# Batch 1's softmax denominators by VectorE's 32x32 turns, in a fused attention and channel-mix kernel with all steps placed anew

## The chip, the cores and the metric

The kernel runs on one core of one Trainium2 chip. The metric is device time in microseconds for one launch, as the median of the runs shown. One further execution was profiled; it has a time of its own.

## What is computed

Eight batches, eight heads, 576 tokens, 64 values a head and 32 memory slots. The reference, cut to what matters:

```python
a = exp(phi - max(phi)); a = a / (sum(a) + 1e-9)          # over the 32 slots
k_m = einsum('bhsm,bhsd->bhmd', a, k)
v_m = einsum('bhsm,bhsd->bhmd', a, v)
scores = q @ k_m.T / sqrt(64)
attn = exp(scores - max(scores)); attn = attn / (sum(attn) + 1e-9)
x = attn @ v_m                                            # heads side by side: 8 x 576 x 512
xk = mu_k * x + (1 - mu_k) * x_prev                       # x_prev: the token before
xr = mu_r * x + (1 - mu_r) * x_prev
h = maximum(xk @ w_k, 0)                                  # 512 -> 1024
out = sigmoid(xr @ w_r) * ((h * h) @ w_v)                 # 1024 -> 512, float32
```

## The kernel before

All work is cut into small steps, and `PLAN` (lines 19 to 39) is a list of them written out by hand, one word for a step. At line 591 the words are turned into calls in exactly that order, so each engine gets its instructions in the order in which the words stand. An instruction that waits holds those behind it on its engine. There is no loop over batches that sets the order: the list mixes steps of several batches.

A word `b:name` is a step of batch `b`. `exp` (L226) is ScalarE's exponential of phi. `z` (L248) sums it over tokens with matmuls and takes the reciprocal. `k`, `v`, `kv` (L238) are the 36 or 72 small matmuls that gather k and v into the 32 slots. `nk`, `nv`, `hn` (L275, L286) scale them, `tk`, `ht` (L307) transpose the keys, `q0`, `q1`, `qh0`, `qh1` (L325) turn q by VectorE in 32x32 blocks, `s` (L340, L345) makes the scores and their exponentials `e`. A number after `exp`, `hn`, `ht`, `qh`, `s`, or a `c` after `k0`, `v0`, picks one half of the heads or of the rows.

Then come the softmax denominators, in one of two ways. The first way has four `l` steps (L355 to L360): a matmul of `e` with a block matrix of ones, `sumh`, sums over the 32 slots of each head and leaves the sum on all 32 rows, and ScalarE takes Ln of it. `h0z` to `h3z` or `r0z`, `r1z` (L365) then take Exp of minus that, which is the reciprocal. The second way has three VectorE steps: `fe` (L370) turns `e` in 32x32 blocks, `fs` (L376, L377) adds over the 32 slots and takes reciprocals, and `fo` (L382) turns these back, each repeated 32 times. In both ways `y0` to `y3` or `w0`, `w1` (L389) multiply `e` by the result. Batches 4 to 7 take the second way before the change, batches 0 to 3 the first.

For batches 2 to 7, `x0`, `x1` make the attention output and `dd`, `k0d`, `r0d` and others mix each token with the one before on VectorE and ScalarE. For batches 0 and 1 the mix is folded into the values instead: `nk0`, `nr0`, `nk1`, `nr1` (L435) scale the values by mu (spread over rows by `mub`, L201 to L205), and `mk0`, `mk1`, `mr0`, `mr1` (L444 to L452) make the mixed inputs by matmuls straight into PSUM. ScalarE and VectorE share their copies out.

The channel mix: `cN:f` (L525 to L533) is one 128-wide block of keys for chunk N of tokens: four matmuls, a relu by ScalarE, a square by VectorE. `g:t` (L548, L553) is the gate of 128 tokens and its exponential. `sg:p` (L559, L560) finishes the sigmoid of two such tiles on ScalarE. `o:t` (L574, L576) is the value product of 128 tokens, VectorE's product with the gate, and the store that SP's queue issues. Chunk 0 and the value tiles 0 to 3 go in halves `a` and `b`.

`0:busyN` issues N matmuls on zeros (L196), whose result nothing reads. The words `p:...` and `b:load` issue loads; all but the first phi go through POOL's queue, in the order of the words. `p:k:0a` and the identity (`PRE`) stand ahead of the list. `b:load` loads batch b+2, and does nothing for 6 and 7. All PSUM tiles share eight banks; `sg` has two buffers, `rl` three.

Of the kernel before, what the change touches and what calls it, by code (L numbers as in the profile page):

```python
# [16 lines left out]


PLAN = [
    "p:k:0b 0:exp0 0:exp1 0:mub 0:mu 0:z 0:k1c 0:k0c 0:hn0 0:hn1 p:q:0a 0:qh0 0:ht0 p:q:0b p:v:0b 0:qh1 0:ht1 p:v:0a",  # L20
    "0:s0 0:l0 0:h0z 0:s1 0:l1 0:v0c 0:y0 0:v1c 0:nr0 0:nk1 0:h1z 0:l2 0:l3 0:nr1 p:wk:4-8 0:h3z 0:y1 0:h2z 0:y3 0:y2",
    "0:busy9 0:nk0 p:wk:0-4 0:mk1 p:phi:1 0:mk0 c0:3b p:wr:0-4 0:mr0 1:exp 0:mr1 c0:3a c0:6b c0:1b c0:4a g:3 c0:2a",
    "c0:5b p:k:1 g:1 g:2 1:k 1:z 1:nk p:q:1 1:q0 sg:1 1:q1 c0:7b c0:6a p:v:1 c0:7a 1:tk g:0 c0:0a c0:0b c0:5a 1:s",
    "c0:2b 1:v c0:1a 1:l2 1:l1 c0:4b 1:h2z 1:nk0 1:h1z p:wv:0-2 1:l3 1:l0 1:y2 p:wv:2-4 1:nr0 1:nr1 o:2a 1:h0z 1:y1",
    "1:h3z sg:0 1:nk1 1:y0 o:3a 1:y3 o:3b o:2b 1:mk1 0:load o:0a 1:mk0 1:mr0 2:exp c1:0 c1:3 g:4 c1:1 1:mr1 c1:7 g:5",
    "2:z sg:2 2:kv 2:nk 2:q1 2:q0 c1:2 2:tk 2:nv 1:load 2:load c1:4 c1:5 o:1b 3:exp c1:6 2:s o:5 2:l1 2:l0 2:l2 2:l3",
    "2:r1z 2:w1 2:r0z 2:w0 3:z o:0b o:4 3:kv 3:nk 3:nv 2:x0 g:7 g:6 3:tk 3:q1 2:x1 3:q0 2:dd sg:3 o:1a g:8 2:k0d",
    "2:k2d 3:s 4:exp o:7 o:6 3:l1 3:l0 2:r0d 7:load 3:l2 c2:2 3:l3 c2:3 3:r0z 3:w0 3:r1z 3:w1 c2:6 c2:0 c2:1 c2:5 4:z",
    "3:x1 2:r2d 4:q1 4:kv 4:ak c2:4 c2:7 3:x0 4:q0 3:load g:9 sg:4 5:exp 3:dd 4:tk 4:av 3:k2d o:8 o:9 3:k0d g:12 g:10",
    "5:z 3:r2d 3:r0d 5:q0 4:s 5:kv 5:ak 4:fe 5:av 5:q1 g:11 c3:3 c3:0 sg:5 4:fs 5:load 7:exp c3:7 4:fo c3:6 4:w0",  # L30
    "4:load c3:4 g:13 4:w1 o:10 c3:2 sg:6 c3:5 7:z c3:1 o:11 4:x0 g:14 7:kv 4:x1 7:ak 7:q0 7:q1 g:15 5:tk 4:dd o:12",
    "4:k2d sg:7 5:s 4:k0d 6:exp o:13 g:16 5:fe 5:fs g:17 5:fo c4:1 7:tk sg:8 o:15 7:av c4:6 c4:5 5:w0 c4:0 c4:3 5:w1",
    "6:z 6:q0 4:r2e 7:s c4:4 7:fe 6:load c4:2 c4:7 o:14 4:r0e 5:x0 o:17 6:kv 6:ak 7:fs 5:x1 5:dd 6:q1 g:18 g:19 sg:9",
    "o:16 5:k0d 6:av g:21 g:20 6:tk 5:k2d 5:r2e o:19 6:s o:18 6:fe 5:r0e 6:fs c5:4 6:fo c5:2 c5:1 sg:10 g:23 6:w1",
    "c5:0 c5:3 6:w0 c5:6 g:22 c5:5 c5:7 6:x1 7:fo o:20 7:w1 6:x0 7:w0 sg:11 o:21 6:dd g:25 6:k2d 6:k0d 7:x1 o:22 7:x0",
    "7:dd 6:r2e o:23 7:k2d g:24 sg:12 6:r0e c6:3 c6:2 c6:4 7:k0d c6:5 g:26 c6:7 c6:0 c6:6 c6:1 g:27 c7:1 c7:6 c7:0",
    "o:24 c7:7 o:25 g:29 7:r2e sg:13 c7:5 7:r0e o:26 c8:4 c8:3 c7:4 c8:5 c8:6 c7:3 g:28 c7:2 o:27 c8:1 sg:14 g:30",
    "g:31 sg:15 o:31 c8:0 o:30 g:32 g:33 o:28 sg:16 c8:2 o:29 c8:7 o:33 g:35 g:34 sg:17 o:32 o:34 o:35",
]

LOADS = {None: ("phi", "k", "v", "q")}
# [589 lines left out]
```

## Time and profile before

| what | us |
|---|---|
| runs shown | 203.63, 204.36, 205.88 (median 204.36) |
| the profiled execution's own time | 204.69 |
| its span, first to last instruction | 202.9 |
| TensorE busy | 188.7 |
| VectorE busy | 143.2 |
| ScalarE busy | 159.9 |
| nine matmuls of `busy9`, from 16.28 | 4.05 |
| first matmul of `mk1` | 20.26 |
| last value tile's matmuls end, in the chain | 199.22 |

The span is measured on the core from its first to its last instruction; the time of the execution holds 1.8 us more. The profile's page has the share of each engine, the span in 40 slices, and the chain of work that ended last. Other views give groups of instructions by line and shape, a timeline, the chain in order of time, busy time in chosen stretches, and for each load the time from its issue to its landing. Matmuls overlap in the records, so the busy time of a group of them is more than the time it keeps the engine.

### The profile page before, as it was taken

How to read it: one execution, taken by the hardware profiler on the slowest of the kernel's cores; microseconds unless marked ns; L12 is line 12 of the kernel's file. 1: busy time of each engine (PE TensorE's matmuls, PEld its weight loads, DVE VectorE, ACT ScalarE, POOL GpSimd, SP SyncE). 2: the span in 40 equal slices, each digit the busy share in tenths (PEclk: the TensorE clock that was granted, in tenths of full speed). 3: DMA queues.
4: the chain of work that ended last, by engine and by line, in shares of the span. 5: the costliest groups of instructions: out<-in, count | busy, mean ns of one | idle time of the engine just before them, and what ended most of it. 6: DMA issues, size and time to landing. Idle time of an engine off the chain costs nothing.

```text
span 202.9 us, 5384 instructions
## 1 busy us (share of the span) xinstructions
PE 188.7 (93%) x2174; PEld 97.5 (48%) x2174; DVE 143.2 (71%) x344; ACT 159.9 (79%) x318; POOL 29.5 (15%) x45
## 2 busy tenths in 40 slices
PE   0459999999999999999999999999999999999992
PEld 0324666755565454544446844444444444444451
DVE  2275746775748999999899989898999732713422
ACT  2235989988968999999999889988999739697360
POOL 7643222201504010036000000000000000000000
PEclk9999999999999999999999999999999999999998
DMA  6999999999999999999999213240422022223435
GB/s 162 169 207 263 209 208 198 267 222 292 212 274 238 243 294 222 240 147 204 257 245 232 60 25 82 52 103 3 103 57 52 3 54 50 52 52 89 98 86 144
DMA packets 24537, 31.29 MB, mean 154 GB/s; under 512 B 1968, under 2 KB 19648, under 8 KB 24512
## 3 DMA queue, kind: packets, MB, share of 16 engines
q0 software_dynamic: 17392, 20.91, 55.4%
q1 hardware_dynamic: 6352, 9.19, 17.9%
q10 hardware_dynamic: 768, 0.85, 1.3%
q8 instruction: 17, 0.28, 0.6%
q14 instruction: 8, 0.07, 0.1%
HBM read 38.28 MB, written 9.44 MB: 235 GB/s over the span
## 4 chain that ended last, share of the span: by engine, by line
PE 91%; DMA 3%; DVE 2%; ACT 1%; issue 1%; POOL 1%; POOLq 0%; DVEq 0%
PE pv L574 31%; PE pk L525 31%; PE pr L548 16%; PE kvps L238 4%; DMA kv<-in_k_dram 3%; PE scps L340 2%; PE idle L196 2%; PE nops L294 2%; PE mxps L294 1%; PE zps L355 1%; PE zps L248 1%; DVE qT L325 1%; DVE o L576 0%; PE ktps L307 0%; ACT e L345 0%
## 5 line engine op out<-in xcount | busy, mean ns | idle before, releaser
L525 PE MATMUL pk<-xkT,wk 128*128 128x512 bf16 (+4 forms) x352 | 68.4, 340 | 0.2 <-ACT xkT L452 0.2
L574 PE MATMUL pv<-wv,sq 128*128 128x512 bf16 (+1 forms) x328 | 67.8, 353 | 0.3 <-DVE sq L533 0.3
L529 ACT ACTIVATE rl<-pk 128x512 bf16<-128x512 f32 (+3 forms) x80 | 41.7, 559 | 10.2 <-PE pk L525 9.0
L525 PEld LDWEIGHTS <-wk 128*128 128x128 bf16 x352 | 33.2, 98 | 28.6 <-issue 1.0
L574 PEld LDWEIGHTS <-sq 128*128 128x128 bf16 x328 | 30.8, 98 | 29.6 <-issue 1.1
L533 DVE TENSOR_TENSOR sq<-rl 128x512 bf16<-128x512 bf16 (+5 forms) x104 | 31.6, 336 | 17.6 <-ACT rl L529 16.9
L576 DVE TENSOR_TENSOR o<-sg,pv 128x512 f32<-128x512 f32 (+1 forms) x41 | 24.9, 616 | 16.1 <-PE pv L574 11.2
L548 PE MATMUL pr<-wr,xrT 128*128 128x512 bf16 x144 | 35.5, 379 | 0.1
L553 ACT ACTIVATE sg<-pr 128x512 f32<-128x512 f32 x36 | 21.2, 609 | 7.0 <-PE pr L548 5.3
L548 PEld LDWEIGHTS <-xrT 128*128 128x128 bf16 x144 | 13.5, 98 | 15.8 <-ACT xrT L452 0.4
L560 ACT ACTIVATE sg<-sg 128x1024 f32<-128x1024 f32 x18 | 19.0, 1058 | 0.6
L559 ACT ACTIVATE sg<-sg 128x1024 f32<-128x1024 f32 x18 | 19.1, 1059 | 0.3
L401 ACT CAST x<-nops 128x320 bf16<-128x320 f32 (+1 forms) x48 | 15.7, 421 | 2.7 <-PE nops L294 2.6
L345 ACT ACTIVATE e<-scps 128x288 bf16<-128x288 f32 x32 | 10.6, 415 | 6.7 <-PE scps L340 6.6
L389 DVE TENSOR_TENSOR atn<-e,lz 128x576 bf16<-128x576 bf16 (+2 forms) x20 | 12.3, 632 | 3.4 <-ACT lz L365 3.4
L325 DVE STREAM_TRANSPOSE qT<-q 128x576 uint32<-128x576 uint32 (+1 forms) x16 | 13.1, 835 | 0.3 <-DMA q<-in_q_dram 0.3
L427 DVE TENSOR_TENSOR xrT<-x,mu_d 128x1152 bf16<-128x1152 bf16 x12 | 9.0, 751 | 3.7 <-ACT mu_d L424 3.4
L424 ACT ACTIVATE mu_d<-diff,mu 128x576 bf16<-128x576 bf16 x16 | 11.6, 783 | 0.0
L226 ACT ACTIVATE em<-ph 128x1152 bf16<-128x1152 f32 (+1 forms) x9 | 9.5, 1061 | 2.5 <-DMA ph<-in_phi_dram 2.5
L238 PE MATMUL kvps<-kv,em 64*32 64x128 bf16 (+1 forms) x720 | 8.6, 218 | 2.2 <-DMA kv<-in_k_dram 2.2
L426 DVE TENSOR_SCALAR mu_d<-diff,mu 128x576 bf16<-128x576 bf16 x32 | 10.2, 362 | 0.0
L238 PEld LDWEIGHTS <-em 64*32 64x32 bf16 x720 | 7.2, 93 | 4.8 <-issue 4.3
(65 smaller groups left out, 146.1 us busy)
## 6 DMA issues: line engine op xcount, KB each, us to landing
out_dram<-o SPq DMA_DIRECT2D x61, 128.0 KB, 2.4
ph<-in_phi_dram POOLq DMA_DIRECT2D x7, 576.0 KB, 17.2
kv<-in_k_dram POOLq DMA_DIRECT2D x7, 576.0 KB, 17.1
q<-in_q_dram POOLq DMA_DIRECT2D x7, 576.0 KB, 19.4
kv<-in_v_dram POOLq DMA_DIRECT2D x7, 576.0 KB, 19.7
out_dram<-o SPq DMA_DIRECT2D x18, 64.0 KB, 5.6
wk<-in_moe_w_k_dram POOLq DMA_DIRECT2D x2, 512.0 KB, 12.6
wv<-in_moe_w_v_dram POOLq DMA_DIRECT2D x2, 512.0 KB, 21.1
```

The costliest lines, as they stand in the source:

```text
L238: nc.tensor.matmul(kvps[c][g * M:(g + 1) * M], lhsT=em[ROWS[c], j, g, :], rhs=kv5[ROWS[c], parts, g, j, :], start=j == 0, stop=j == NJ - 1 ...
L325: nc.vector.transpose(dst.bitcast(U32), src.bitcast(U32))
L401: nc.scalar.copy(st["x"][:, i, sl], pss[i])
L525: nc.tensor.matmul(pk[:, p0 - lo:p1 - lo], lhsT=wk_sb[:, di, fi * 128:(fi + 1) * 128], rhs=xk_T[:, di, p0 % RING:p0 % RING + p1 - p0], sta ...
L529: nc.scalar.activation(rl, pk, AF.Relu)
L533: nc.vector.tensor_mul(sq[:, fi, p:p + p1 - p0], rl[:, p0 - lo:p1 - lo], rl[:, p0 - lo:p1 - lo])
L548: nc.tensor.matmul(pr, lhsT=xr_T[:, di, c0:c0 + 128], rhs=wr_sb[:, di, :], start=(di == 0), stop=(di == ND - 1))
L553: nc.scalar.activation(sg[:, t % 2], pr, AF.Exp, scale=-1.0)
L559: nc.scalar.activation(gated[p], gated[p], AF.Ln, bias=1.0)
L560: nc.scalar.activation(gated[p], gated[p], AF.Exp, scale=-1.0)
L574: nc.tensor.matmul(pv[:, cols], lhsT=sq[:, fi, p:p + 128], rhs=wv_sb[:, fi, cols], start=(fi == 0), stop=(fi == NF - 1))
L576: nc.vector.tensor_mul(o[:, cols], gated[t // 2][:, t % 2, cols], pv[:, cols])
```

## The change

Batch 1's four `l` and four `hNz` steps are gone, and `1:fe`, `1:fs`, `1:fo` stand in the list instead; its `y0` to `y3` stay. `0:busy9` has become `0:busy4`. All the other words are the same ones, in a new order. Nothing but `PLAN` is touched. The list at its start and its end:

```diff
-    "p:k:0b 0:exp0 0:exp1 0:mub 0:mu 0:z 0:k1c 0:k0c 0:hn0 0:hn1 p:q:0a 0:qh0 0:ht0 p:q:0b p:v:0b 0:qh1 0:ht1 p:v:0a",
-    "0:s0 0:l0 0:h0z 0:s1 0:l1 0:v0c 0:y0 0:v1c 0:nr0 0:nk1 0:h1z 0:l2 0:l3 0:nr1 p:wk:4-8 0:h3z 0:y1 0:h2z 0:y3 0:y2",
-    "0:busy9 0:nk0 p:wk:0-4 0:mk1 p:phi:1 0:mk0 c0:3b p:wr:0-4 0:mr0 1:exp 0:mr1 c0:3a c0:6b c0:1b c0:4a g:3 c0:2a",
-    "c0:5b p:k:1 g:1 g:2 1:k 1:z 1:nk p:q:1 1:q0 sg:1 1:q1 c0:7b c0:6a p:v:1 c0:7a 1:tk g:0 c0:0a c0:0b c0:5a 1:s",
-    "c0:2b 1:v c0:1a 1:l2 1:l1 c0:4b 1:h2z 1:nk0 1:h1z p:wv:0-2 1:l3 1:l0 1:y2 p:wv:2-4 1:nr0 1:nr1 o:2a 1:h0z 1:y1",
-    "1:h3z sg:0 1:nk1 1:y0 o:3a 1:y3 o:3b o:2b 1:mk1 0:load o:0a 1:mk0 1:mr0 2:exp c1:0 c1:3 g:4 c1:1 1:mr1 c1:7 g:5",
...
-    "o:24 c7:7 o:25 g:29 7:r2e sg:13 c7:5 7:r0e o:26 c8:4 c8:3 c7:4 c8:5 c8:6 c7:3 g:28 c7:2 o:27 c8:1 sg:14 g:30",
-    "g:31 sg:15 o:31 c8:0 o:30 g:32 g:33 o:28 sg:16 c8:2 o:29 c8:7 o:33 g:35 g:34 sg:17 o:32 o:34 o:35",
+    "0:exp0 p:k:0b p:q:0b 0:exp1 0:k0c 0:z 0:hn0 p:q:0a p:phi:1 1:exp 0:k1c 0:ht0 p:v:0b 0:mu p:v:0a 0:mub 0:hn1",
+    "0:qh1 0:ht1 0:s1 0:qh0 0:s0 0:v1c 0:l0 0:v0c 0:nk0 0:h0z 0:l1 0:y0 1:z 0:l3 0:l2 0:nk1 0:busy4 0:nr1 0:nr0 0:h1z",
+    "0:y1 0:h3z 0:h2z p:k:1 0:y3 0:y2 0:mk1 0:mk0 p:wk:4-8 p:wk:0-4 1:k 1:nk p:q:1 p:wr:0-4 0:mr1 c0:5a c0:6a c0:7b",
+    "0:mr0 p:wv:2-4 c0:3a c0:1b p:v:1 1:tk c0:3b c0:7a 1:q1 c0:6b p:wv:0-2 1:q0 c0:0b c0:4a 0:load c0:1a c0:2a c0:4b",
+    "1:s 1:fe 1:fs c0:0a g:1 c0:2b 1:fo g:0 c0:5b sg:0 g:3 g:2 1:y1 sg:1 2:exp o:1b 1:v 1:nr0 1:nr1 1:y0 1:y2 1:nk0",
+    "1:y3 o:3b 1:nk1 7:load o:2b o:3a o:2a 1:mr0 1:mk1 g:5 2:z 1:load 1:mk0 g:4 c1:3 c1:7 c1:4 c1:5 sg:2 2:kv 2:nk",
+    "2:nv 1:mr1 2:q0 2:q1 c1:1 2:tk c1:0 c1:2 c1:6 2:s o:4 2:l3 2:l2 2:l1 2:l0 2:r1z 2:w1 2:load 2:r0z 2:w0 o:0a",
...
+    "7:r2e o:27 o:26 c7:1 c7:4 o:24 c8:0 c8:3 c8:6 c7:2 g:28 c8:4 g:31 g:30 g:29 sg:14 c8:5 c8:1 o:29 c8:2 o:28 g:32",
+    "g:33 c8:7 sg:16 o:32 o:33 g:35 sg:15 o:31 g:34 sg:17 o:30 o:34 o:35",
```

## The prediction

> **What bounds the kernel now.** I read the busy table first, then the slices, then the chain of waits, because a busy share alone doesn't say whether an engine sets the end.
>
> ```profile
> PE 188.7 (93%) x2174; PEld 97.5 (48%) x2174; DVE 143.2 (71%) x344; ACT 159.9 (79%) x318; POOL 29.5 (15%) x45
> PE   0459999999999999999999999999999999999992
> PE 91%; DMA 3%; DVE 2%; ACT 1%; issue 1%; POOL 1%; POOLq 0%; DVEq 0%
> ```
>
> TensorE is full from the fourth slice (15 us) to the last, and the chain is TensorE for 91%. So a change can gain in two ways only: less work on TensorE, or fewer places where it stood still or did nothing of use. The chain in order of time (start, length, what) shows both near its start:
>
> ```profile
> 16.49 3.84 PE idle L196 x9
> 20.33 0.43 PE mxps L294 x13
> 20.76 0.37 ACT xkT L452
> ...
> 36.30 0.27 ACT rl L529
> 36.57 0.07 issue
> 36.63 0.71 ACT lz L360 x2
> 37.34 0.29 ACT rl L529
> 37.62 0.02 issue
> 37.65 0.30 DVE sq L533
> ```
>
> 3.84 us are filler (busy9). After it, useful work runs from 20.33 to the last matmul's end at 199.22. In that run the pieces that aren't TensorE's add up to 2.9 us as far as the end of batch 2's 2:kv (50.30), and to nearly nothing behind. TensorE did some 1.15 us of work inside them (two 256-column sums 0.21, four half-width value matmuls 0.43, some 0.5 of mixes), so about 1.75 us were lost: 0.4 at 20.8, 1.1 at 36 to 38 and the rest at 42.6. The middle one is the change's target: ScalarE makes relus and batch 1's Ln there while keys wait. Busy by stage (TensorE, weight loads, VectorE, ScalarE, POOL):
>
> ```profile
> 25.00:30.00 5.00, 4.98 (x105) 3.10 (x106) 1.97 (x8) 4.07 (x10) 1.48 (x2) 1.00 1.21 208
> 30.00:35.00 5.00, 4.98 (x92) 3.08 (x92) 3.95 (x11) 4.79 (x12) 1.50 (x2) 1.00 1.39 200
> 35.00:40.00 5.00, 4.66 (x101) 3.68 (x101) 2.97 (x11) 4.55 (x14) 1.48 (x2) 1.00 1.25 267
> ```
>
> ScalarE is at 13.4 of 15 us, VectorE at 8.9.
>
> **What the Trainium skill says.** "TensorE: Matmul & The Clock Gate", section "What's actually happening": the array runs at half clock until it has been busy for one window of about 3.4 us, and the windows run free of the program. The trace agrees: the nine 512-column fillers start 0.427 us apart, later 512-column keys 0.216, and the rate changes at about 20.2. The same page, "Architectural detail": ScalarE and VectorE take their instructions strictly in order, so a step that waits holds all behind it. "VectorE: DVE Perf Modes", "The perf-mode tier table": a reduction has no fast mode; here 1152 elements take 1.347 us, against 0.751 for an add of as many. "DMA: Bandwidth & Descriptors", "Anatomy of one DMA": about 2.0 us plus bytes at 436 GB/s. The landings agree: a 590 KB half load follows the one before by 1.45 us, 407 GB/s.
>
> **Part 1, the denominators.** Rows of the groups by form (mean ns of one):
>
> ```profile
> L370 DVE STREAM_TRANSPOSE eT<-e 128x576 uint32<-128x576 uint32 x4 | 3.1, 763 | 0.0
> L376 DVE TENSOR_REDUCE se<-eT 128x36 f32<-128x1152 bf16 x4 | 5.4, 1347 | 0.0
> L377 DVE RECIPROCAL se<-se 128x36 f32<-128x36 f32 x4 | 1.5, 378 | 0.1
> L382 DVE STREAM_TRANSPOSE lz<-se 128x1152 f32<-128x1152 f32 x4 | 5.5, 1381 | 0.0
> L360 ACT ACTIVATE lz<-zps 128x320 f32<-128x320 f32 x8 | 3.3, 453 | 0.5 <-PE zps L355 0.5
> L360 ACT ACTIVATE lz<-zps 128x256 f32<-128x256 f32 x8 | 3.1, 392 | 0.5 <-PE zps L355 0.5
> ```
>
> Removed: TensorE 2 x 0.133 + 2 x 0.107 = **0.48 us**, on the path. ScalarE 2 x (0.453 + 0.392) of Ln and, from their rows, 2 x (0.470 + 0.417) of Exp = 3.46 us, in its fullest stage. Four PSUM banks go. Added: VectorE 0.763 + 1.347 + 0.378 + 1.381 = 3.87 us, of the 6.1 it had free there.
>
> Which wait comes next? I walk VectorE's new order from batch 1's scores: exponentials ready at about 32.5; fe and fs until 35.0; two squares that waited behind them, 35.6; fo 37.0; a square and y1, 37.7; then an output, two value scalings, y0, y2, a scaling, y3, outputs 3b, 2b, 3a, 2a: 42.5. TensorE reaches 1:mr0 and 1:mk1 at 40.9. Their eight PSUM banks are those of these outputs, so they end at 42.75 and not 41.8: **0.95 us** of a new VectorE wait for the 1.75 of old ones. If my start is late, both move together.
>
> **Part 2, the start.** TensorE can't begin mk1 before all four y of batch 0. Landings first: in the trace k 7.5 and 8.9, q 10.3 and 11.9, v 13.3 and 14.8, wk 17.3 and 19.8, phi1 21.4, wr 24.9, k1 27.7, q1 30.5, v1 33.3, wv 36.1 and 38.7. They land in the order of POOL's issues, and each issue (0.74 us) waits for the landing eight before. With the same gaps the new order gives q 10.3 and 11.9, phi1 13.4, v 14.8 and 16.3, k1 19.1, wk 21.6 and 24.2, q1 27.0, wr 29.6 to 30.5, wv 32.5, v1 35.3, wv 38.0. POOL pays no more issues. SP's stores change order, not number; nothing but stores queues behind them.
>
> Two waits are new. 1:exp now stands on ScalarE ahead of batch 0's exponentials and waits for phi1: 13.4 to 14.6. And mub (1.19 us of TensorE, 0.84 of VectorE) comes after k0c, k1c and ht0, not at 5.2, so that hn1, both 1.37 us turns of q, ht1 and both scores stand behind it: copies end at 12.15, s1 starts at 14.15, s0 at 15.5. The exponentials of s0 end at 17.0 (15.6 before for the second), v0 and the sums follow, ScalarE does its eight Ln and Exp until 20.9, the last y ends at 21.4. In the trace the last y ended at 18.4 and the last scaling at 18.6, and filler hid 1.7 us. So mk1 starts at 21.45, not 20.33: **+1.1 us**. Batch 1's sums (1:z, 0.25 us) have then been done in waiting time: **-0.25**. With busy4, five fillers (2.1 us) go, which is worth nothing here: they never stood on work.
>
> Landings then cost nothing: c0:5a is reached at 23.6 (wk 21.6), 3a at 25.6 (24.2), g:1 at 31.5 (30.5), 1:v at 36.7 (35.3). Each cover is 1 to 2 us; an earlier start eats it.
>
> The clock is the unknown. Four fillers cover half a window, and 0.55 us of nothing follows before mk1. If the clock rises one window after the fillers' start at 19.2 with a bad phase, about 24, then mk1, mk0, 1:k and mr1 run slowly for 2.5 us, a third of it lost: **+0.9**. Bounds: 0 (warm at 20.9) and +2.6 (down until keys are dense and a window more, about 27). The window from 13.3 to 16.7 had about 2.7 us of streaming and did not raise it.
>
> **Part 3, the rest.** From 70 to 160 us ScalarE has 84 and VectorE 84.5 us of work for TensorE's 90, and the chain shows no wait. A new order of the same work can hardly gain there. Bounds 0 to 2; I take **+0.2**. At the end three value tiles (5.2 us) cover the last gate's 2.7 us of ScalarE; without this cover it would cost up to 1.
>
> **The sum**, against the profiled execution (span 202.9, own time 204.69): -0.48 - 1.75 - 0.25 + 1.1 + 0.95 + 0.9 + 0.2 = +0.67, so 205.3. That execution stands 0.33 above the median of 204.36; for the median I say **205.0**.
>
> **Rivals.** (B) Slower: the clock stays at half because busy4 is too short; the point that decides is a rate change later than about 26. Then +2.6 for 0.9: 206.7. For it speaks the early window; against it that windows from 17.5 on are about 85% full. (C) Faster: mk1 starts at 20.4, the clock rises in time, and VectorE's chain is out of the way: -0.48 - 1.75 - 0.25 + 0.2 + 0.2 = -2.1, so 202.3. For it: ScalarE's relief is real and my walk is strict. (D) The new order opens waits after 50 us by ScalarE or VectorE backlog, 2 us: 206.8. That the change isn't made can't be: the steps are in the list by name.
>
> **Chances.** The forecast 0.45, B 0.25, C 0.20, D 0.10. About 1% (2 us) is what a measurement tells from no change. Faster than 202.3: most of C's lower half and a little, 0.14. Over 206.4: two thirds of B, half of D, a little of the first, 0.23. Same 0.63. The range 203.0 to 207.0 takes in B and D and half of C.
>
> **What would show it.** mk1's start (21.45); the spacing of c0:5a's matmuls (0.135 warm, twice that cold) and when it changes; ScalarE gone from the chain at 36 to 38; VectorE's outputs in the chain at 41 to 43; 2:kv ending near 50.5; no waits after. I am wrong if mk1 starts by 20.4, or if the chain after 50 us holds over 1 us that isn't TensorE's.

## The result, and the profile after

| | before | after |
|---|---|---|
| median of 20 runs each, side by side, us | 204.52 (203.49 to 206.12) | 205.44 (204.40 to 207.73) |
| profiled execution: its own time, its span | 204.69, 202.9 | 206.03, 204.3 |
| TensorE, VectorE, ScalarE busy | 188.7, 143.2, 159.9 | 186.9, 146.4, 157.6 |
| `mk1` starts (end of the fillers) | 20.33 | 21.46 |
| end of the last value tile's matmuls | 199.22 | 200.54 |

The ratio is 1.005, with a 95% interval from 1.0032 to 1.0069; it is taken over all fast executions (207.73 is a slow one and stays out), so it isn't quite that of the two medians. The changed kernel is slower by about 0.9 us. That is clear of the noise, but less than the 1% that the prediction took for no change. From the page of the changed kernel, the busy table, TensorE's slices, one of the DMA queues (packets, MB, share of 16 engines) and the chain by engine:

```profile
PE 186.9 (92%) x2165; PEld 97.4 (48%) x2165; DVE 146.4 (72%) x348; ACT 157.6 (77%) x310; POOL 29.3 (14%) x45
PE   0537969999999999999999999999999999999992
q8 instruction: 17, 0.28, 0.5%
PE 88%; DMA 6%; POOL 2%; issue 1%; ACT 0%; DVE 0%; POOLq 0%
```

ScalarE and VectorE have all but left the chain, as the change's idea demands. TensorE has less work and the span is longer all the same. The sixth slice (25.5 to 30.6 us), which read 9 before, reads 6. Busy time by stage of the changed kernel, with the columns as in the prediction:

```profile
25.00:30.00 5.00, 3.38 (x49) 2.41 (x48) 2.71 (x9) 2.64 (x7) 1.48 (x2) 1.00 1.28 204
35.00:40.00 5.00, 5.00 (x101) 3.17 (x100) 4.89 (x10) 4.63 (x9) 0.00 (x0) 1.00 1.26 266
```

The stage from 35 to 40 us has come from 4.66 to 5.00 us of TensorE, and VectorE from 2.97 to 4.89. That is the change as meant. But in the stage from 25 to 30 TensorE does 3.38 us of work, where it did 4.98. The chain in order of time (start, length, what) shows the place:

```profile
19.76 1.71 PE idle L196 x4
21.46 1.22 PE mxps L294 x28
22.68 0.78 PE kvps L238 x72
23.46 0.41 PE mxps L294 x16
23.87 1.21 PE pk L525 x8
25.08 0.02 issue
25.10 0.83 ACT rl L529 x2
25.93 1.44 issue
27.37 0.48 PE mxps L294 x10
```

Ahead of 27.37 stand 1.44 us of "issue": the engine stands still, and the profile shows nothing that it waits for. All behind 44.04 is TensorE's, to the last matmul. TensorE's timeline there (start, length, tile, and in brackets how long it had been idle and for what):

```profile
25.43 0.32 PE L294 MATMUL mxps<-atn,vm 32*64 32x320 bf16 x1
27.37 0.48 PE L294 MATMUL mxps<-atn,vm 32*64 32x320 bf16 x23 [1.62 <-issue]
```

`mr0` has issued one of its matmuls, and the next comes 1.94 us later. An operand that isn't ready would have held the first one as well. The second one writes another PSUM bank, so a bank could hold it alone; but the last thing that the chain shows ahead of it, ScalarE's relus, was over at 25.93, and 1.44 us are left.

Stage lengths from the chains serve to compare the kernels. The start of `mk1` shifts between executions of one kernel, so lengths say more than times. (In before and in e5_bfold, batch 1's `mr1`, 0.35 us, stands inside the second stretch; in the others it stands in the third.)

| kernel | `mk1` starts | second stretch: from there to the end of `2:kv` | third stretch: from there to the last matmul |
|---|---|---|---|
| before | 20.33 | 29.96 | 148.92 |
| after | 21.46 | 29.82 | 149.26 |
| after again (e1) | 19.93 | 29.79 | 149.30 |
| e2_swap | 20.29 | 32.75 | 149.27 |
| e3_klate | 21.12 | 28.94 | 149.27 |
| e4_mubearly | 20.70 | 29.78 | 149.30 |
| e5_bfold | 20.18 | 33.84 | 148.95 |
| e7_aln | 20.93 | 32.33 | 149.64 |
| e9_pad75 | 21.43 | 27.76 | 150.40 |
| e10_pad32 | 20.39 | 30.19 | 149.28 |
| e11_best2 | 20.00 | 29.07 | 149.29 |

### The profile page after: what moved, and what is told of

It is laid out like the page before. It is cut to its first block, busy times and chain, and to the rows that moved or that the text cites. A ratio compares the mean times of both kernels' runs of the same rounds, so it can differ in the third digit from the quotient of the medians.

```text
span 204.3 us, 5362 instructions
## 1 busy us (share of the span) xinstructions
PE 186.9 (92%) x2165; PEld 97.4 (48%) x2165; DVE 146.4 (72%) x348; ACT 157.6 (77%) x310; POOL 29.3 (14%) x45
## 4 chain that ended last, share of the span: by engine, by line
PE 88%; DMA 6%; POOL 2%; issue 1%; ACT 0%; DVE 0%; POOLq 0%
PE pv L574 31%; PE pk L525 31%; PE pr L548 16%; DMA kv<-in_v_dram 6%; PE kvps L238 3%; PE mxps L294 2%; PE nops L294 2%; PE scps L340 1%; POOL kv L111 1%; PE zps L355 1%; PE idle L196 1%; PE zps L248 1%; POOL q L111 1%; PE ktps L307 0%; ACT rl L529 0%
## 5 line engine op out<-in xcount | busy, mean ns | idle before, releaser
L525 PE MATMUL pk<-xkT,wk 128*128 128x512 bf16 (+4 forms) x352 | 67.4, 340 | 0.0
L574 PE MATMUL pv<-wv,sq 128*128 128x512 bf16 (+1 forms) x328 | 66.8, 353 | 0.0
L529 ACT ACTIVATE rl<-pk 128x512 bf16<-128x512 f32 (+3 forms) x80 | 42.2, 561 | 10.4 <-PE pk L525 8.9
L553 ACT ACTIVATE sg<-pr 128x512 f32<-128x512 f32 x36 | 21.9, 611 | 8.5 <-PE pr L548 8.2
L238 PE MATMUL kvps<-kv,em 64*32 64x128 bf16 (+1 forms) x720 | 9.2, 219 | 8.6 <-DMA kv<-in_k_dram 7.5
L238 PEld LDWEIGHTS <-em 64*32 64x32 bf16 x720 | 7.7, 96 | 11.9 <-issue 6.3
```

Of the source, the lines that this page charges most:

```text
L238: nc.tensor.matmul(kvps[c][g * M:(g + 1) * M], lhsT=em[ROWS[c], j, g, :], rhs=kv5[ROWS[c], parts, g, j, :], start=j == 0, stop=j == NJ - 1 ...
L525: nc.tensor.matmul(pk[:, p0 - lo:p1 - lo], lhsT=wk_sb[:, di, fi * 128:(fi + 1) * 128], rhs=xk_T[:, di, p0 % RING:p0 % RING + p1 - p0], sta ...
L529: nc.scalar.activation(rl, pk, AF.Relu)
L553: nc.scalar.activation(sg[:, t % 2], pr, AF.Exp, scale=-1.0)
L574: nc.tensor.matmul(pv[:, cols], lhsT=sq[:, fi, p:p + 128], rhs=wv_sb[:, fi, cols], start=(fi == 0), stop=(fi == NF - 1))
```

## The experiments

The kernel before stands beside each group of experiments: its median is 204.28 us beside e1 to e4, 204.18 beside e5 to e8 and 204.11 beside e9 to e11. The ratios are to these, so kernels of different groups compare better by ratio than by time. The diffs show only the words of the list around each change.

**What stops TensorE at 25.4?** The trace holds the packets of the queue named "instruction" in the page: 17 of 16,384 bytes each. TensorE has 2 x 2165 recorded instructions (matmuls and weight loads), 255 for each packet, so I take these as TensorE's program, in pieces of about that many instructions. (The division is rough: e9 below has 2 x 2240 and the same 17 packets, so 264 each, and what was loaded ahead of the first packet isn't counted.) The Trainium skill, "Runtime: NRT & Kernel Launch", section "Instruction fetch mechanics", gives 256 instructions for a piece of this size and says that the cost of crossing from one piece to the next is "mostly hidden"; the stop of 1.94 us looked at here isn't hidden. In the changed kernel it comes after TensorE's 705th recorded instruction (four semaphore instructions counted with them), and one piece lands at 25.99, in the stop. Theory F: TensorE runs out of instructions, since some 200 of them are used up between 22.6 and 25.4. Rival: `mr0` waits for something of its own.

e1_again is the changed kernel once more, without an edit.

> The changed kernel once more. Its first profile holds a stop of TensorE from 25.4 to 27.4 us, of which the chain puts 1.44 us to nothing that it can name. Theory fetch: TensorE ran out of instructions, since a 16 KB piece of its program was asked for during the burst of small matmuls of 1:k, lay behind the loads, and landed at 26.0 only; then the stop is there again, at the same place give or take 20 instructions, 1.5 to 2.2 us long, after that piece lands. Theory accident: it was a hiccup of that one execution; then no stop over 1 us between 21 and 50 us, and a span near 202.9. Time in both: 205 to 206, 1.003 to 1.007 of before.

205.49 us, ratio 1.0063 [1.0035, 1.0090]. The whole start lay 1.5 us earlier in this execution, but the stop was 1.92 us, after the same 705th instruction. So it belongs to the kernel, and the start's 1.5 us don't.

e2_swap moves `mr0` ahead of three blocks of keys:

```diff
-0:mr1 c0:5a c0:6a c0:7b 0:mr0 p:wv:2-4
+0:mr1 0:mr0 c0:5a c0:6a c0:7b p:wv:2-4
```

> 0:mr0 stands before c0:5a, c0:6a, c0:7b and not behind them. Theory fetch: the stop sits at the same count of TensorE instructions (about 705), so in the middle of mr0 or in the first key behind it, starts near 24.2, lasts about 3 us and ends near 27.4; the time is that of the changed kernel within 0.4 (205.4). Theory wait (mr0's second matmul waits for a PSUM bank or another engine that the records hide): mr0 no longer follows the relus, no stop over 1 us there, time 1.4 us less than the changed kernel (204.0).

208.31 us, ratio 1.0199 [1.0150, 1.0248]. The chain:

```profile
22.20 1.34 PE mxps L295 x25
23.54 2.54 issue
26.08 0.33 PE mxps L295 x8
26.41 4.28 PE pk L526 x20
```

The stop is no longer at the step's second matmul but 13 matmuls deep inside `mr0` (29 behind `1:k`), again after 705 instructions: F, not the rival. The time was not what I expected from a mere shift. The stop is longer (2.81 us from start to start), and after it 20 matmuls of keys take 4.28 us where the same 20 take 1.63 + 1.09 = 2.72 in e9's chain: 1.6 us by the half clock. The first few are still about 0.14 apart, then those of 320 columns 0.267, and the trace's clock records have half clock from 26.95 to 30.36.

e3_klate takes the 144 short instructions of `1:k` (0.78 us for 72 matmuls and their loads) out of the rush:

```diff
-0:mk0 p:wk:4-8 p:wk:0-4 1:k 1:nk p:q:1
+0:mk0 p:wk:4-8 p:wk:0-4 p:q:1
...
-c0:1b p:v:1 1:tk c0:3b
+c0:1b p:v:1 1:k 1:nk c0:3b 1:tk
```

> 1:k and 1:nk (144 small TensorE instructions in 0.8 us) stand behind c0:1b and not ahead of mr1. Theory fetch: without the burst the piece of program is there before it is used, or nearly; the stop of 2 us at mr0 shrinks to the 0.6 us of its wait for a relu, and what is left of it, under 1 us, moves into 1:k. Time about 1 us less than the changed kernel (204.4). Theory wait: mr0 follows the same three keys, so the stop of 2 us stays there and the time stays at 205.4.

204.66 us, ratio 1.0013 [0.9988, 1.0037], 0.8 us less than the changed kernel. The second stretch is 0.85 us shorter, and what is left of the stop lies inside `1:k`:

```profile
26.28 0.42 PE kvps L239 x41
26.70 0.13 issue
26.83 0.48 PE kvps L239 x31
```

That confirms F a second time: `mr0` has none of the stop now, and whatever comes 706th gets what is left of it, 0.32 us from start to start.

e9_pad75 and e10_pad32 put 75 and 32 two-column matmuls on zeros at the very front, in the time in which TensorE waits for the first loads (`0:pad75` or `0:pad32` ahead of `0:exp0`; their results go to a PSUM tile that nothing reads). They change the count at which each step stands (and move every later PSUM tile by one bank, in both alike):

```diff
+    def pad(n):
+        ps = psum.tile([128, 2], F32, name="padps", tag="ps", bufs=8)
+        for _ in range(n):
+            nc.tensor.matmul(ps, lhsT=zeros, rhs=zeros[:, 0:2], start=True, stop=True, skip_group_check=True)
```

> The changed kernel with 75 more matmuls of two columns on zeros (150 TensorE instructions, nobody reads them) ahead of all else, in the 6 us in which TensorE waits for the first load. Nothing else moves. Theory fetch: only the count of instructions matters. The piece that is asked for at the 504th instruction is now asked for before the fillers, near 18.5 and not in 1:k at 22.6, so it can be used near 23.2; the stop falls to under 0.6 us, sits inside 1:k, and the time falls by 0.8 to 1.4 us, to 204.4, though work was added. Theory wait (the stop belongs to mr0 and what stands before it): stop at mr0 as it was, time 205.5 or more.

> The same with 32 such matmuls (64 instructions). Theory fetch: now the count of 705 falls on the end of 1:k (at 641 of the changed kernel's own), which is reached near 23.3, and the piece can be used near 26.3 only: a stop of 2.5 to 3 us at the end of 1:k or the start of mr1, and keys at half clock behind it as in the swap; time 1 to 3 us above the changed kernel, 206.5 to 208.5. Theory wait: no difference from the changed kernel, 205.5.

With 75, 205.26 us, ratio 1.0041 [1.0023, 1.0059]. The stop is gone (0.04 us at the 705th), and the stretch from `mk1` to the end of `2:kv` is 27.76 us against 29.82 and 29.79: **2.05 us less, with the same steps in the same order**. (Some 0.2 of that lie ahead of `1:k`, which e9 reaches 1.05 us after the start of `mk1`, against 1.22 and 1.29.) The median fell by only 0.2, and the table says where half of the gain went: the third stretch grew by 1.1 us. VectorE's waits in a window from 96 to 112 us (line, in all, times, longest), first of the changed kernel and then of e9:

```profile
DVE qT L325 <- DMA q<-in_q_dram: 1.5, 1, 1.5
```

```profile
DVE qT L330 <- DMA q<-in_q_dram: 2.8, 1, 2.8
```

VectorE's turn of batch 7's q waits for its transfer in both. After, these 1.5 us touch nobody; in e9, where all is needed 2 us earlier and the transfer lands only 0.8 us earlier (101.6 against 102.4), they become 2.8 us, and the keys behind them wait: of the 10 us from 100 to 110 TensorE is busy for 9.16, after for 10.00. So half of what the stop's removal gave was paid back at another wait. That is one profiled execution, in which the loads ran late from the start (phi1 at 15.2 us, in e1 at 13.7). Where the rest of the gain went, some 0.7 us of the median, isn't shown.

With 32, 204.71 us, ratio 1.0026 [1.0008, 1.0044], where I expected a longer stop and a slower kernel. That was wrong. The piece came at 21.38, earlier than after's by 4.6 us, and the pause was 0.70 us from start to start, inside `1:k`. So when a piece is asked for can't be read from the count alone. Its chain:

```profile
22.42 0.47 issue
22.90 0.24 PE kvps L243 x3
23.14 0.58 PE mxps L299 x11
23.72 3.02 PE pk L532 x12
```

The 12 matmuls of keys take 0.25 each, half speed, where the changed kernel's took 0.15. The clock did not fall there: in this execution it had not risen yet. The 40 matmuls of `mk1` and `mk0` took 1.36 us (0.70 at full clock), and the trace's first record of full clock is at 26.53, in the changed kernel's at 22.48. Whether the pause kept it from rising isn't shown. The slow keys cost about 1.4 us (3.02 against 1.63 in e9), so this execution's 30.19 in the table doesn't price the pause alone.

One rule holds in all of them. The landing of the second of the 17 packets and the starts of TensorE's 705th and 706th instructions, counted from each trace (us):

```
kernel          piece landed   705th   706th   landing to 706th
before             23.28       28.77   28.77        5.49
after              25.99       25.43   27.37        1.38
e1_again           24.46       23.89   25.81        1.35
e2_swap            24.66       23.27   26.08        1.42
e3_klate           25.55       26.51   26.83        1.28
e4_mubearly        25.20       24.67   26.57        1.37
e7_aln             25.51       25.09   26.84        1.33
e8_best            22.68       24.52   24.53        1.85
e9_pad75           21.38       22.66   22.70        1.32
e10_pad32          21.38       22.20   22.90        1.52
e11_best2          24.24       25.66   25.66        1.42
```

In these 11 executions the 706th never starts sooner than 1.28 us after the landing, whatever instruction it is, and where the 705th is early it waits 1.28 to 1.52 us from the landing. (In e5 and e6, below, the piece was there 4.8 and 6.2 us ahead.)

**What holds the start?** The prediction named the late place of `mub`. e4_mubearly puts it back near its old place:

```diff
-0:exp1 0:k0c
...
-0:mu p:v:0a 0:mub 0:hn1
+0:exp1 0:mub 0:mu 0:k0c
...
+p:v:0a 0:hn1
```

> 0:mub and 0:mu stand ahead of 0:k0c again, so that hn1 and both turns of q don't stand behind mub's copies. Both theories: mk1 starts about 1 us earlier, near 20.4. Theory start (the late mk1 is what costs, as the prediction's sum has it with +1.1): time 1 us less than the changed kernel, 204.4. Theory fetch: the piece of program still lands near 26 and the stop still ends near 27.4, so it grows by about what the start gains, 2.5 to 3 us, and the time falls by under 0.4 (205.2).

205.44 us, ratio 1.0064 [1.0043, 1.0085]: no gain, and the stop, 1.90 us, has not grown as theory F had it. Ahead of batch 0's exponentials its chain has `1:exp`, which starts when phi1 lands (14.5). So the place of `mub` was covered by that wait. The cover is thin: in e2 and e3, where phi1 landed at 14.01 and 14.57, the chain goes through `mub`'s copies, and the exponentials end 0.1 and 0.3 us later than phi1 alone would have it (its landing, 1.16 us of `1:exp`, 1.21 of exponentials; an estimate from e4's chain). In the changed kernel's first execution it is neither of them: the chain goes back to the second half of v, which landed at 18.00 where the prediction had 16.3 and e1 16.36. That `1:exp` alone is to blame was not tried by itself; e8 below moves it with other steps.

e6_bbusy4 is the kernel before with `0:busy4` for `0:busy9`.

> The kernel before with busy4 for busy9, nothing else. Theory waste (filler beyond the operands' arrival at 18.6 us stands on the path): mk1 starts near 18.7 and the time falls by 1 us or more, 203.2. Theory clock (the filler also raises the clock): mk1 and the first keys run at half speed, matmuls of 320 columns 0.27 us apart and not 0.135, until 22 us or later; gain 0 to 0.5, 203.9 to 204.4.

204.31 us, ratio 1.0003 [0.9982, 1.0023]. The five fillers are worth nothing as time. They did stand ahead of work, though: `mk1` starts at 17.69, 2.6 us earlier (about 1 us of it because the last `y` was done earlier in this execution, at 17.4 and not 18.4). TensorE then waits 1.27 us for wk, and the 16 matmuls of keys that took 2.12 us before take 3.45, with half clock in the trace's records from 20.64 to 24.05.

**What are the denominators worth?** e5_bfold does that part alone: the kernel before, with only its `l` and `h` words replaced.

```diff
-1:s c0:2b 1:v c0:1a 1:l2 1:l1 c0:4b 1:h2z 1:nk0 1:h1z p:wv:0-2 1:l3 1:l0 1:y2 p:wv:2-4
+1:s c0:2b 1:v c0:1a 1:fe c0:4b 1:fs 1:nk0 p:wv:0-2 1:fo 1:y2 p:wv:2-4
```

(`1:h0z` and `1:h3z`, a few words further on, go as well.)

> The kernel before with one part of the change alone: batch 1's l and h steps out, fe, fs, fo in at their places, nothing else moved. Theory placement (the denominators gain 0.5 us of TensorE and the 1.1 us wait at 36 to 38 us, but VectorE's chain of about 9 us from the exponentials to the last y is too long for the little work that stands between 1:s and 1:mk1 in the old order): the chain gets a VectorE wait of 2 to 3 us ahead of 1:mk1, near 42 us; time 0.5 to 1 us above the kernel before, 205.0. Theory part (the denominators alone are a gain, the rest of the change spoils it): no such wait, 203.0.

208.54 us, ratio 1.0217 [1.0191, 1.0243]: 4.4 us slower than before, where I had expected 0.5 to 1. From 36.2 to 43.6 the chain is VectorE's; some of its pieces:

```profile
36.51 0.69 DVE eT L371
37.37 1.27 DVE se L377
38.67 0.38 DVE se L378
39.22 1.29 DVE lz L383
```

With the old order the four new instructions stand in front of the value scalings and the outputs, and TensorE has too little work ready behind them. The wait also costs the clock: the trace has half clock from 43.42 to 46.84, and eight half-width value matmuls there take 1.82 us, before 0.99.

e7_aln undoes that part alone: the changed kernel, with matmuls, Ln and Exp put back where the `f` steps stood.

```diff
-1:s 1:fe 1:fs c0:0a g:1 c0:2b 1:fo g:0 c0:5b sg:0
+1:s c0:0a 1:l2 1:l1 g:1 1:h2z 1:h1z c0:2b 1:l3 1:l0 g:0 c0:5b 1:h3z 1:h0z sg:0
```

> The changed kernel with batch 1's denominators by ones matmuls, Ln and Exp again (l2, l1 behind c0:0a, then h2z, h1z, l3, l0, h3z, h0z), all else as changed. Theory gain (in the new order they are worth TensorE's 0.48 us and part of a ScalarE wait): 0.5 to 1.3 us above the changed kernel, 206.3, with ScalarE in the chain between 33 and 42 us. Theory nothing (VectorE's load takes it back): within 0.3 of the changed kernel, 205.5.

207.56 us, ratio 1.0160 [1.0130, 1.0189]: 2.1 us over the changed kernel, where I expected 0.5 to 1.3. ScalarE holds the chain from 33 to 44 us, here around the first Exps:

```profile
38.50 0.66 ACT lz L366 x2
39.17 0.95 ACT sg L560
40.14 1.06 ACT sg L561
```

So in the new order the denominators gain 2.1 us over the old steps at the places that I gave them there, and in the old order they cost 4.4. The two parts of the change can't be judged one by one.

**Is there a better version?** e8_best is the changed kernel with the start mended: `mub` and `mu` early, wk's loads ahead of phi1's, `1:exp` behind `0:mr1`, `1:z 1:k 1:nk` behind `c0:1b`, and six fillers.

```diff
-0:exp1 0:k0c 0:z 0:hn0 p:q:0a p:phi:1 1:exp 0:k1c 0:ht0 p:v:0b 0:mu p:v:0a 0:mub 0:hn1
+0:exp1 0:mub 0:mu 0:k0c 0:z 0:hn0 p:q:0a 0:k1c 0:ht0 p:v:0b p:v:0a p:wk:4-8 p:wk:0-4 p:phi:1 0:hn1
...
-0:y0 1:z 0:l3 0:l2 0:nk1 0:busy4
+0:y0 0:l3 0:l2 0:nk1 0:busy6
...
-0:mk0 p:wk:4-8 p:wk:0-4 1:k 1:nk p:q:1 p:wr:0-4 0:mr1 c0:5a
+0:mk0 p:q:1 p:wr:0-4 0:mr1 1:exp c0:5a
...
-c0:1b p:v:1 1:tk c0:3b c0:7a 1:q1
+c0:1b p:v:1 1:z 1:k 1:nk c0:3b c0:7a 1:tk 1:q1
```

> A version of my own: the changed kernel's list, but mub and mu early, v and wk loaded ahead of phi1 and k1, 1:exp behind 0:mr1, 1:z, 1:k and 1:nk behind c0:1b, busy6. Batch 0's exponentials no longer stand behind 1:exp, and the burst of 1:k comes late. Theory fetch and start: mk1 near 19.4, no stop over 1 us up to 28 us, time 1.5 to 2.2 us below the kernel before, 202.4. Rival (the filler's end leaves TensorE at half clock, or keys wait for wk): 203.5 to 204.3.

**203.28 us, ratio 0.9959 [0.9945, 0.9973]: faster than both kernels**, by 0.4% and about 1%, between the two expectations. `mk1` starts at 18.29, the 40 matmuls of `mk1` and `mk0` take 0.70 us (1.29 in the changed kernel), and there is no stop. It loses about 1 us at 23.2, where ScalarE has `1:exp` and five relus in the chain. From the first matmul of `mk1` to the end of the last value tile's it takes 179.1 us and the changed kernel 179.2, so in its profile the gain is the earlier start: behind `mk1` TensorE stands idle for 1.45 us in four waits, where the changed kernel has 1.62 us in the one stop.

e11_best2 is e8 with `1:exp` behind the three blocks of keys and `1:z 1:k 1:nk` one block later.

> My own version with 1:exp behind the relus of c0:5a, 6a and 7b, and 1:k one key later, since in its profile ScalarE stood at 1:exp waiting for phi1 until 20.9 and the relus behind it held TensorE's banks for 1 us near 24. If this wait reaches the end: 0.3 to 0.8 us below e8_best, 202.7. If the landing of q for batch 2 near 50 us sets the end of this stage, as that version's chain says: no difference, 203.3.

203.47 us, ratio 0.9964 [0.9950, 0.9978], no difference from e8.

## Why the prediction came out as it did

The predicted time (205.0 against 205.44), the range and the call of a change under 1% held. They held by luck: four terms were too large by about 1.8 us together (the start 0.4, VectorE's wait 0.9, the clock 0.3, part 3 0.2), and a stop of about 2 us had no term.

- **Removed ScalarE wait** (the -0.48 and the -1.75): right in place. ScalarE has left the chain at 36 to 38. e7 measures the part as 2.1 us; the two terms came to 2.2. They aren't the same waits (e7's stand from 33 to 44 us in the new order, and 0.4 of the 1.75 stood at 20.8, ahead of any denominator of batch 1), so the closeness proves little.
- **The late start** (+1.1, `mk1` at 21.45): measured 21.46 in the first execution and 19.93 in the next, so the agreement to a hundredth is luck; by the prediction's own sign, "I am wrong if mk1 starts by 20.4", the second execution speaks against it. The medians differ by 0.92, of which the stretches behind `mk1` make about 0.2, so the start's share is about 0.7, by subtraction. Of its two causes, `mub` gains nothing alone (e4); phi1's landing holds the start in e1 and e4, and the first execution's 21.46 came from v's landing, which the prediction had 1.7 us too early.
- **VectorE's new wait** (+0.95): mis-sized. In the chain there is at most 0.04 us of it, at 44.00. I walked VectorE's instructions end to end and got 10.0 us from the scores to the last output; it took 9.2, and TensorE, held up before, came later.
- **The clock** (+0.9): mis-sized. The 40 matmuls of `mk1` and `mk0` took 1.29 us instead of 0.70, about 0.6; the keys at 23.9 were at full speed, and the trace's first record of full clock is at 22.48, where the prediction had about 24.
- **Part 3** (+0.2): nothing. The third stretch is 149.26 less the 0.35 of `mr1`, so 148.91, against 148.92 before.
- **"They never stood on work", of the five fillers**: right as to time, wrong as a reason in the order before, where `mk1` started earlier without them (e6). In the new order no run took them alone.
- **The loads' rate**, on which no term rests: 590 KB is what a half load reads. The page counts the 288 KB that it writes, and by these the 1.45 us between landings are 203 GB/s. So the agreement that the prediction states holds for the bytes read only.
- **What the sum had no term for**: the instruction supply. Behind `mk1` the prediction's terms are -0.48 - 1.75 - 0.25 + 0.95 + 0.9 = -0.63, and with the measured sizes of the last two (0.04 and 0.6) -1.84. Measured was 29.82 + 0.35 - 29.96 = +0.21. The 2.05 that are missing are the stop: 1.94 us in its trace, 1.85 to 2.05 by e9. The step that failed is the one that costs `1:k`, `mk1`, `mk0` and `mr1` at their streaming time only and moves them together into 21 to 24 us: e3 and e9 show that what that crowding costs is the piece of program that isn't there yet.

So the gain of the denominators was real, some 2 us, and was given back by the stop and by the late start. Two things stay open: why the boundary shows after 705 recorded instructions rather than 768 (three pieces; not every instruction need be in the trace), and when a piece is asked for. In the changed kernel the packet started at 25.04, 2.4 us after the 504th instruction; in e10 it started 0.14 after it, in before 0.51. Nor is it shown that the loads hold it up: the packet itself took 0.9 to 1.0 us in every execution.

## What to carry to other kernels

Count instructions as well as microseconds when many tiny matmuls are moved together: 144 instructions in 0.78 us use up the program faster than it came here, and an "issue" wait in the chain at the same instruction count in every variant is its mark. Judge a new algorithm for a step with the order that suits it, since the same step was worth 2.1 us in one order and cost 4.4 in the other. When a stop goes, look at which transfer was just in time: e9 gained 2.05 us by 50 us and lost 1.1 of it to a load at 101.

## What the runs showed that was not expected

- A fetch of TensorE's program can stop it for 1.9 us (after, e1, e4) to 2.8 us (e2), so here it wasn't hidden. In the changed kernel it is the only one of the 17 packets that does: behind `mk1` TensorE has no other idle time over 0.1 us. The following instruction started 1.28 us or more after the packet's landing.
- The clock fell after pauses shorter than one window. The Trainium skill, "TensorE: Matmul & The Clock Gate", section "What's actually happening", has it fall after an idle window of about 3.4 us; here it fell after a pause of 2.54 us (e2), and after pauses of 0.48 and 1.27 us close together (e6), each time for 3.41 us. The changed kernel's stop, 1.62 us of idle time, left it at full speed: the keys behind it are 0.136 apart. What share of a window has to be busy no run here settles.
- Executions of one kernel differ by 1.5 us in when the first loads are done (19.93 and 21.46 for `mk1`), with the same length behind it to 0.04 us. v's second half landed at 18.00 in the one and 16.36 in the other.
